# Scalings of k and q on GpSimd from slot 10 on, each as two instructions of 256 columns in place of one of 512

## The chip, the cores and the metric

The kernel runs on one core of a Trainium2 chip. The metric is the device time of one execution in microseconds, as the median of several runs; lower is better. The engines are named as in the profile: PE is TensorE (matmuls), PEld its weight loads, DVE is VectorE, ACT is ScalarE, POOL is GpSimd, SP is the engine whose queue issues nearly all the transfers.

## The reference

The input is q, k and v of shape (4, 8, 768, 64) (batch, heads, sequence, head dimension), and three weight matrices in float32. First a retention layer with a decay per head, then a bilinear feed-forward block:

```python
gamma = 1.0 - 2.0 ** (-5.0 - np.arange(H, dtype=np.float32))
for t in range(S):
    state = gamma * state + outer(k[:, :, t], v[:, :, t])
    y[:, :, t] = scale * (q[:, :, t] @ state)
...
x = y.transpose(0, 2, 1, 3).reshape(3072, 512)
out = ((x @ w_a) * (x @ w_b)) @ w_out      # 512 -> 1536 -> 512
```

## The kernel before, in words

**Tiling.** The 4 x 768 positions are cut into 24 slots of 128 positions. The decay is split into a factor for each position of k and one for each position of q (tables `ktab` and `qtab`, computed once), so that a slot needs: scaled and cast copies of k and q (`kqb`, bf16), a cast of v (`vb`), the transposes of `kqb` (`kqT`), the scores with their mask (`aT`), the running state (`sums`, cast to `gst`), and the output `xt`, which is the input of the feed-forward block. The feed-forward works on blocks J = 0 to 7 of 4, 2, 2, 2, 2, 4, 4 and 4 slots.

**One block.** For each of twelve slices `ft` of 128 hidden columns TensorE computes `a` (line 598) and `g` (line 610), ScalarE casts `a` to `asb` (line 602), and VectorE multiplies `g` by `asb` into `ht` (line 613). Blocks 2 to 7 then compute the output product by a scheme with fewer matmuls (`ffn_fast`, matmuls at line 772), for which four sums and differences of parts of `ht` are formed: `hsum` (line 670), both inputs in SBUF, 128x256 or 128x512 bf16. VectorE does these in blocks 2 to 5 and partly later, GpSimd does most of them in blocks 6 and 7. The results leave PSUM through `snap` (ScalarE, line 784) and `osb` (VectorE, lines 787 and 820). Blocks 6 and 7 use such a scheme for `a` too: it needs combinations of the weights, `ta`, which GpSimd forms after the last slot's casts (line 690) and TensorE reads at line 712, and combinations of `xt`, `xs` (line 681, VectorE).

**Order.** Every engine's instructions are chained in the order in which the program emits them, so each engine works through a fixed list. The recurrence of later slots is put into the blocks by a table of visits, `ahead`: `(casts, t)` emits the casts of slot t, and `(turn, new, old)` the state updates and scores of two new slots (lines 287 and 317) and the outputs of two old ones (lines 359 and 371). For GpSimd only the order of its own list counts, and the waits for data and buffers.

**Casts of one slot** (`casts`, line 246): GpSimd scales k, then q, by `scaled` (the instruction at line 239); SP issues the transpose of both (line 252); after an odd slot SP issues the loads of the next pair of slots, k and q of both and then v of both (lines 96 and 98); last GpSimd casts v (line 204). All loads and transposes stand in SP's one queue, in this order. The raw loads have three buffers of two slots, `kqb` and `vb` six buffers of one slot.

**One scaling** works on 128 partitions x 512 columns, which are 8 heads x 64. The source holds the heads in order (two halves r of four heads hp); the destination interleaves the halves, hp before r, so that the transposes come out as the scores need them. The factor is one number for each partition and head, broadcast over the 64 columns. The first slots, up to 9, are scaled by `casts2` and `casts` in the same way, some of them on VectorE.

Of the kernel before, what the change touches and what calls it, by code (L numbers as in the profile page):

```python
# [12 lines left out]
ALU = mybir.AluOpType  # L13
# [14 lines left out]
def kernel(  # L28
# [46 lines left out]
    def seq(bi):  # L75
        ins = bi.ins
        prev = last.get(ins.engine)
        if prev is not None:
            tc.add_manual_dep(ins, prev.name, nosync, reason="program order")
        last[ins.engine] = ins  # L80
        return bi
# [151 lines left out]
    def scaled(eng, t, i):  # L233
        ktab, qtab = tabs[0] if t < 2 * PAIRS else tabs[1]
        dst, src, tab = kqb[t][:, i], raws["kq"[i], t], (ktab, qtab)[i][:, t % NCH]
        dst = dst.rearrange("p hp r d -> p r hp d")
        src = src.rearrange("p (r hp) d -> p r hp d", r=2)
        tab = tab.rearrange("p (r hp) o -> p r hp o", r=2).to_broadcast([P, 2, HP, D])
        seq(eng.tensor_tensor(dst, src, tab, op=ALU.mult))  # L239

    def new_nat(t):
        kqb[t] = nat.tile([P, 2, HP, 2, D], BF16, tag="kqb", name="kqb")
# [3 lines left out]
    def casts(t, names="kqv"):  # L246
        if "k" in names:
            new_nat(t)
            scaled(nc.gpsimd, t, 0)
            scaled(nc.gpsimd, t, 1)  # L250
            kqT[t] = tra.tile([P, 2, HP, P], BF16, tag="kqT", name="kqT", bufs=6)
            seq(nc.sync.dma_start_transpose(
                out=kqT[t].rearrange("p a b c -> p (a b) c"),
                in_=kqb[t].rearrange("p a hp r d -> p (a hp r d)")))
            if t % 2 and t + 1 < NSLOT:
                for names in ("kq", "v"):
                    load_slot(t + 1, names)
                    load_slot(t + 2, names)
        if "v" in names:
            cast(nc.gpsimd, vb[t], raws["v", t])  # L260
# [169 lines left out]
    def casts2(u, on):  # L430
        if 2 * u not in kqb:
            for t in (2 * u, 2 * u + 1):
                new_nat(t)
        for (i, par), eng in on.items():
            t = 2 * u + par
            if i == V:
                cast(eng, vb[t], raws["v", t])
            else:
                scaled(eng, t, i)
# [631 lines left out]
```

## Time and profile before

| | |
|---|---|
| median of 3 runs | 221.41 us (221.08 to 221.74) |
| profiled execution | 221.99 us, span 220.3 us |
| PE busy | 212.1 us (96%) |
| DVE busy | 147.8 us (67%) |
| POOL busy | 116.2 us (53%), 157 instructions |
| ACT busy | 96.6 us (44%) |
| scalings on POOL, k and q | 21 + 21 of 128x512, 22.7 + 22.5 us, mean 1081 and 1076 ns |
| adds of `hsum` on DVE, largest group | 32 instructions, 14.2 us, mean 450 ns |

Times of rows are microseconds from the start of the span unless marked ns. A timeline row gives the start, the time it took (of a merged row, of all its instructions together), the engine, the line, the operation with output and inputs, and in brackets how long the engine idled before it and what ended that. SPq is SP's issue queue. Matmuls overlap, so a row of several is shorter than the sum of their durations. In a row of groups stand busy time, mean ns of one, and idle time before.

### The profile page before, as it was taken

The numbers are of one execution on the slowest core, as the hardware profiler recorded it, in microseconds if no ns is written. First come the engines' busy times: TensorE is split into PE (matmuls) and PEld (weight loads), VectorE is DVE, ScalarE is ACT, GpSimd is POOL, SyncE is SP. The second block draws the span as 40 slices with busy tenths as digits, with TensorE's granted clock in tenths as the row PEclk, the third lists the DMA queues.
The fourth block names the chain that finished last, engine by engine and source line by source line (L and its number), as shares of the span: only waits on it lengthen the run. The fifth ranks groups of instructions, "written<-read, shape, count | busy, mean of one in ns | idle before, by whom it ended". The sixth has DMA issues, their size and how long they took to land.

```text
span 220.3 us, 7032 instructions
## 1 busy us (share of the span) xinstructions
PE 212.1 (96%) x2875; PEld 156.5 (71%) x2875; DVE 147.8 (67%) x324; ACT 96.6 (44%) x240; POOL 116.2 (53%) x157
## 2 busy tenths in 40 slices
PE   8889999999999999999999999999999999999993
PEld 7568898886456888887878445478666478666682
DVE  2774456657806687698685489897877694777731
ACT  3665334442426436426466343636432643443231
POOL 6457798682734545054352514536959960087500
PEclk9999999999999999999999999999999999999999
DMA  6999999997999997997868899898800002200022
GB/s 172 346 377 382 369 299 390 342 207 167 216 259 246 233 220 141 128 236 203 191 130 201 230 150 257 156 221 120 237 0 4 0 3 98 97 0 1 3 95 95
DMA packets 94832, 39.77 MB, mean 181 GB/s; under 512 B 76112, under 2 KB 91728, under 8 KB 94800
## 3 DMA queue, kind: packets, MB, share of 16 engines
q1 hardware_dynamic: 94656, 39.20, 70.2%
q8 instruction: 22, 0.36, 0.7%
q10 hardware_dynamic: 144, 0.13, 0.2%
q14 instruction: 10, 0.08, 0.1%
HBM read 28.31 MB, written 6.29 MB: 157 GB/s over the span
## 4 chain that ended last, share of the span: by engine, by line
PE 86%; DVE 5%; DMA 3%; issue 2%; POOL 1%; ACT 1%; SPq 0%; DVEq 0%; POOLq 0%; ACTq 0%
PE g L610 27%; PE a L598 22%; PE o L772 18%; PE o L647 7%; PE a L712 5%; DMA kf<-in_k_dram 3%; DVE ht L613 2%; DVE hsum L670 1%; PE st L287 1%; POOL kqb L239 1%; PE y L359 1%; PE y L371 1%; PE at L317 1%; PE tp L450 1%; PE st L491 1%
## 5 line engine op out<-in xcount | busy, mean ns | idle before, releaser
L613 DVE TENSOR_TENSOR ht<-g,asb 128x256 bf16<-128x256 f32 (+1 forms) x98 | 53.7, 548 | 39.1 <-PE g L610 29.3
L610 PE MATMUL g<-xt,wb_bf 128*128 128x256 bf16 (+1 forms) x432 | 77.7, 308 | 0.3 <-ACT asb L602 0.3
L598 PE MATMUL a<-xt,wa_bf 128*128 128x256 bf16 (+1 forms) x368 | 60.8, 296 | 0.1
L602 ACT CAST asb<-a 128x256 bf16<-128x256 f32 (+1 forms) x82 | 36.8, 450 | 51.4 <-PE a L598 50.8
L610 PEld LDWEIGHTS <-wb_bf 128*128 128x128 bf16 x432 | 42.1, 98 | 16.5 <-issue 0.4
L598 PEld LDWEIGHTS <-wa_bf 128*128 128x128 bf16 x368 | 35.4, 98 | 12.1
L239 POOL TENSOR_TENSOR kqb<-kf,ktab 128x512 bf16<-128x512 f32 x21 | 22.7, 1081 | 40.5 <-DMA kf<-in_k_dram 29.8
L239 POOL TENSOR_TENSOR kqb<-qf,qtab 128x512 bf16<-128x512 f32 x21 | 22.5, 1076 | 6.4 <-DMA qf<-in_q_dram 6.4
L204 POOL CAST vb<-vf 128x512 bf16<-128x512 f32 x24 | 14.8, 624 | 17.8 <-DMA vf<-in_v_dram 13.0
L772 PEld LDWEIGHTS <-hsum 128*128 128x128 bf16 x216 | 21.0, 98 | 4.1 <-DVE hsum L670 0.9
L784 ACT COPY snap<-o 128x256 f32<-128x256 f32 x34 | 12.7, 374 | 21.3 <-PE o L772 19.5
L772 PE MATMUL o<-wt_bf,hsum 128*128 128x256 bf16 x162 | 19.8, 272 | 0.9 <-DVE osb L787 0.5
L670 POOL TENSOR_TENSOR hsum<-ht 128x256 bf16<-128x256 bf16 (+1 forms) x15 | 11.0, 733 | 17.9 <-DVE ht L613 17.9
L772 PEld LDWEIGHTS <-ht 128*128 128x128 bf16 x162 | 15.4, 98 | 2.6
L647 PE MATMUL o<-wo_bf,ht 128*128 128x512 bf16 x72 | 16.1, 379 | 0.0
L670 DVE TENSOR_TENSOR hsum<-ht 128x256 bf16<-128x256 bf16 (+1 forms) x32 | 14.2, 450 | 0.3
L301 DVE TENSOR_TENSOR sums<-st,sums 128x256 f32<-128x256 f32 x30 | 12.7, 423 | 1.5
L772 PE MATMUL o<-wo_bf,ht 128*128 128x256 bf16 x108 | 13.3, 273 | 0.0
L202 ACT CAST gst<-sums 128x256 bf16<-128x256 f32 x33 | 12.6, 412 | 0.5 <-DVE sums L299 0.3
L647 PEld LDWEIGHTS <-ht 128*128 128x128 bf16 x72 | 6.9, 98 | 7.9
L323 DVE TENSOR_TENSOR aT<-at,mask 128x512 bf16<-128x512 f32 x18 | 12.1, 680 | 0.0
L787 DVE TENSOR_TENSOR osb<-o,snap 128x256 f32<-128x256 f32 x20 | 8.3, 416 | 4.8 <-PE o L772 3.2
(99 smaller groups left out, 260.4 us busy)
## 6 DMA issues: line engine op xcount, KB each, us to landing
out_dram<-osb SPq DMA_DIRECT2D x11, 512.0 KB, 3.2
kf<-in_k_dram SPq DMA_DIRECT2D x18, 256.0 KB, 3.9
qf<-in_q_dram SPq DMA_DIRECT2D x36, 128.0 KB, 3.8
vf<-in_v_dram SPq DMA_DIRECT2D x18, 256.0 KB, 4.2
wsta<-in_moe_w_a_dram SPq DMA_DIRECT2D x6, 512.0 KB, 7.6
wstb<-in_moe_w_b_dram SPq DMA_DIRECT2D x6, 512.0 KB, 7.8
wsto<-in_moe_w_out_dram SPq DMA_DIRECT2D x6, 512.0 KB, 8.7
kf<-in_k_dram SPq DMA_DIRECT2D x3, 512.0 KB, 6.1
```

Source lines behind the costliest of these rows:

```text
L202: seq(nc.scalar.copy(dst, src))
L204: seq(engine.tensor_copy(dst, src))
L239: seq(eng.tensor_tensor(dst, src, tab, op=ALU.mult))
L301: seq(nc.vector.tensor_tensor(new, u[c][:, s], old, op=ALU.add))
L598: seq(nc.tensor.matmul(a[:, b0 - c0 : b1 - c0], wa_bf[:, kt, fs], xcols(J, kt, b0, b1), start=(kt == 0 and b0 == c0), stop=(kt == KT - 1 a ...
L602: seq(nc.scalar.copy(asb, a))
L610: seq(nc.tensor.matmul(g[:, b0 - c0 : b1 - c0], wb_bf[:, kt, fs], xcols(J, kt, b0, b1), start=(kt == 0 and b0 == c0), stop=(kt == KT - 1 a ...
L613: seq(nc.vector.tensor_tensor(ht[J][:, ft, c0:c1], g, asbs.pop((J, ft, c0)), op=ALU.mult))
L647: seq(nc.tensor.matmul(o, ht[J][:, ft, i * P : (i + 1) * P], wo_bf[:, f, 2 * r : 2 * r + 2, :].rearrange("p a d -> p (a d)"), start=(ft == ...
L670: seq(eng.tensor_tensor(s[which], x(), y(), op=op))
L772: seq(nc.tensor.matmul(R[:, :DH], lhs, (wo_bf, wt_bf)[w][:, f, m, :], start=(first and f == 0), stop=(f == NH - 1), skip_group_check=True))
L784: seq(nc.scalar.copy(snap[:, i], R[:, :DH]))
```

## The change

From slot 10 on each scaling is issued as two instructions, one for each half r of the heads: four heads, 256 columns. The views are the ones that the single instruction used, with the index r taken out. Both functions that emit casts call `scaled`, but `casts2` handles only slots 0 to 5, so the 14 slots 10 to 23, with two scalings each, are affected: 28 instructions become 56. The engine, the order, the number of elements, the transposes and the loads stay as they were.

```diff
         dst = dst.rearrange("p hp r d -> p r hp d")
         src = src.rearrange("p (r hp) d -> p r hp d", r=2)
         tab = tab.rearrange("p (r hp) o -> p r hp o", r=2).to_broadcast([P, 2, HP, D])
-        seq(eng.tensor_tensor(dst, src, tab, op=ALU.mult))
+        if t < 10:
+            seq(eng.tensor_tensor(dst, src, tab, op=ALU.mult))
+        else:
+            for r in range(2):
+                seq(eng.tensor_tensor(dst[:, r], src[:, r], tab[:, r], op=ALU.mult))
```

## The prediction

> **What bounds the kernel now.** I read the page first (busy times, then the chain that ended last), then a table of windows for TensorE's idle time, then the timeline where it idles.
>
> ```profile
> PE 212.1 (96%) x2875; PEld 156.5 (71%) x2875; DVE 147.8 (67%) x324; ACT 96.6 (44%) x240; POOL 116.2 (53%) x157
> ...
> PE g L610 27%; PE a L598 22%; PE o L772 18%; PE o L647 7%; PE a L712 5%; DMA kf<-in_k_dram 3%; DVE ht L613 2%; DVE hsum L670 1%; PE st L287 1%; POOL kqb L239 1%; PE y L359 1%; PE y L371 1%; PE at L317 1%; PE tp L450 1%; PE st L491 1%
> ```
>
> TensorE is the bound, 212.1 of 220.3 us. GpSimd has half its span free, so its own work is not the point. What the change can win is TensorE's idle time where the scalings of slots 10 to 23 run, from about 66 to 153 us. The windows that hold nearly all of it (columns: window, its length, then TensorE, weight loads, DVE, ACT and POOL busy us with counts, clock, DMA share, GB/s):
>
> ```profile
> 93.00:97.00 4.00, 3.69 (x51) 3.09 (x48) 3.58 (x9) 1.68 (x5) 2.09 (x2) 1.00 1.05 235
> 97.00:102.00 5.00, 4.63 (x142) 3.90 (x143) 4.69 (x12) 2.44 (x7) 3.27 (x4) 1.00 0.88 234
> ...
> 109.00:116.00 7.00, 6.73 (x170) 5.54 (x172) 6.27 (x16) 4.07 (x13) 3.68 (x5) 1.00 0.71 147
> ...
> 144.00:150.00 6.00, 5.51 (x156) 4.58 (x155) 5.32 (x13) 1.78 (x6) 2.17 (x2) 1.00 1.05 237
> ```
>
> Idle: 0.31 + 0.37 us around the end of block 3, 0.27 in block 4, 0.49 at the end of block 5; the granted clock is 1.00 throughout, so nothing here is throttling. The timeline of the first place, all engines:
>
> ```profile
> 90.74 0.28 DVE L670 TENSOR_TENSOR hsum<-hsum,ht 128x256 bf16<-128x256 bf16 x1
> ...
> 93.74 1.04 POOL L239 TENSOR_TENSOR kqb<-kf,ktab 128x512 bf16<-128x512 f32 x1 [5.72 <-DMA kf<-in_k_dram]
> 93.84 1.09 DVE L670 TENSOR_TENSOR hsum<-ht 128x256 bf16<-128x256 bf16 x1
> ...
> 94.77 1.06 POOL L239 TENSOR_TENSOR kqb<-qf,qtab 128x512 bf16<-128x512 f32 x1
> ...
> 95.19 0.79 DVE L670 TENSOR_TENSOR hsum<-hsum,ht 128x256 bf16<-128x256 bf16 x1
> ...
> 96.99 0.45 PE L287 MATMUL st<-vb,kqb 64*64 64x64 bf16 x32 [0.31 <-DVE ht L613]
> ...
> 98.76 1.04 POOL L239 TENSOR_TENSOR kqb<-kf,ktab 128x512 bf16<-128x512 f32 x1
> ...
> 99.27 0.68 DVE L670 TENSOR_TENSOR hsum<-ht 128x256 bf16<-128x256 bf16 x1
> ...
> 99.76 1.09 POOL L239 TENSOR_TENSOR kqb<-qf,qtab 128x512 bf16<-128x512 f32 x1
> ...
> 99.98 1.01 DVE L670 TENSOR_TENSOR hsum<-hsum,ht 128x256 bf16<-128x256 bf16 x1
> ...
> 101.06 1.15 PE L772 MATMUL o<-wt_bf,hsum 128*128 128x256 bf16 x8 [0.37 <-DVE hsum L670]
> ```
>
> See how an add of `hsum` that meets nothing takes 0.28 us, and how one that starts inside a scaling ends just after it: 93.84 + 1.09 = 94.93, when the scaling from 93.74 ended at 94.78; 95.98 against 95.83; 99.95 against 99.80; 100.99 against 100.85. The add is held until the GpSimd instruction is over, then needs 0.15 us more. It is let in even though the next scaling stands ready and starts at 94.77. TensorE then waits for the products of these adds (101.06), or for the `ht` behind them in VectorE's order (96.99). The second place:
>
> ```profile
> 145.26 1.04 POOL L239 TENSOR_TENSOR kqb<-kf,ktab 128x512 bf16<-128x512 f32 x1 [4.77 <-PE o L772]
> ...
> 145.30 1.15 DVE L670 TENSOR_TENSOR hsum<-hsum,ht 128x256 bf16<-128x256 bf16 x1
> ...
> 146.76 1.12 POOL L239 TENSOR_TENSOR kqb<-qf,qtab 128x512 bf16<-128x512 f32 x1 [0.45 <-DMA qf<-in_q_dram]
> 146.90 1.33 DVE L670 TENSOR_TENSOR hsum<-ht 128x256 bf16<-128x256 bf16 x2
> ...
> 148.56 0.41 DVE L787 TENSOR_TENSOR osb<-o,snap 128x256 f32<-128x256 f32 x1
> ...
> 149.02 1.47 PE L772 MATMUL o<-wt_bf,hsum 128*128 128x256 bf16 x12 [0.49 <-DVE osb L787]
> ```
>
> Here the held adds push back `osb` at 148.56, which has to free a bank before TensorE goes on at 149.02.
>
> **The change, part by part.** It removes 28 scalings of 512 columns (slots 10 to 23, k and q) and adds 56 of 256. Same bytes, same order, no new wait, no DMA issue moved; the transposes behind them on SP still wait for the last instruction of q.
>
> *Price of one split.* The trace has no scaling of 256 columns. The nearest rows are two-input adds on POOL in both sizes:
>
> ```profile
> 166.84 1.15 POOL L670 TENSOR_TENSOR hsum<-ht 128x512 bf16<-128x512 bf16 x1
> 167.95 1.15 POOL L670 TENSOR_TENSOR hsum<-ht,hsum 128x512 bf16<-128x512 bf16 x1
> ...
> 169.81 0.67 POOL L670 TENSOR_TENSOR hsum<-hsum,ht 128x256 bf16<-128x256 bf16 x1
> 170.44 0.67 POOL L670 TENSOR_TENSOR hsum<-ht 128x256 bf16<-128x256 bf16 x1
> ```
>
> Start to start 1.11 us for 512 columns and 0.63 for 256, so two halves cost 1.26 - 1.11 = 0.15 more; I take 0.14, as the next add follows 0.62 later. Bounds: 0 below (time by columns alone), and 0.19 above, by the rows' own durations (2 x 0.67 - 1.15). A scaling is 1.00 start to start (85.43 to 86.43 below), so a half is about 0.57. In all 28 x 0.14 = 3.9 us more on POOL, which has 104 us free.
>
> [...]
>
> *Where the price lands.* The scalings sit in a loop that paces itself:
>
> ```profile
> 84.86 0.61 POOL L204 CAST vb<-vf 128x512 bf16<-128x512 f32 x1 [2.37 <-DMA vf<-in_v_dram]
> 85.43 1.04 POOL L239 TENSOR_TENSOR kqb<-kf,ktab 128x512 bf16<-128x512 f32 x1
> 86.43 1.04 POOL L239 TENSOR_TENSOR kqb<-qf,qtab 128x512 bf16<-128x512 f32 x1
> ...
> 87.50 1.23 SPq L252 DMA_TRANSPOSE kqT<-kqb  x1
> ...
> 88.78 1.96 SPq L98 DMA_DIRECT2D kf<-in_k_dram  x1
> ```
>
> The cast of the even slot's v waits for its load; the odd slot's k and q follow (85.43, 86.43); when q ends at 87.47, SP issues the transpose (87.50), and then the loads of the next pair (88.78), for which POOL waits (93.74, 5.72 us). The even slot's splits hide in the wait for v, the odd slot's do not: each round is 0.28 us longer. Slots 10/11 to 22/23 make seven rounds, so slot 14's scalings start 2 x 0.28 = 0.56 us later, slot 22's 6 x 0.28 = 1.7, and what follows slot 23 on POOL, the `ta` combinations, 7 x 0.28 = 1.96. Is that covered?
>
> ```profile
> 153.46 0.67 POOL L690 TENSOR_TENSOR ta<-wa_bf 128x256 bf16<-128x256 bf16 x1
> ...
> 156.36 0.84 POOL L690 TENSOR_TENSOR ta<-wa_bf 128x256 bf16<-128x256 bf16 x1
> ...
> 157.83 0.38 PE L712 MATMUL a<-xs,ta 128*128 128x256 bf16 x2
> ...
> 160.86 0.38 PE L712 MATMUL a<-xs,ta 128*128 128x256 bf16 x2
> ```
>
> The first combination is ready at 154.13 and used at 157.83, that of the next block at 157.20 and used at 160.86: slack 3.7 us. A lag of 1.96 plus a TensorE that arrives 0.9 earlier uses 2.9 of it. Cost: nothing, with 0.8 left; without that cover each us of lag is one of TensorE.
>
> *What it gives back.* A held add waits for the rest of a half, not of a whole. All the held adds shown began in the first half of a scaling: after 0.10, 0.42, 0.51 and 0.22 us at the first place, 0.04 and 0.14 at the second. Each would get free 1.00 - 0.57 = 0.43 earlier: 4 x 0.43 = 1.7 us of VectorE at the first place, 2 x 0.43 = 0.86 at the second, more than the 0.68 and 0.49 that TensorE idles. But the lag changes who meets whom. At the first place the scalings move back 0.56 us: the add of 93.84 then runs free, and the later ones meet other halves. I take two thirds of the 0.68 idle: 0.45. At the second place slot 22's scalings move to about 147.0 and 148.5, behind most of the adds: I take all 0.49. Block 4's 0.27 I leave. Bounds: 0 if the meetings only move; at the top all 1.17 plus the matmul tails that the windows count as busy:
>
> ```profile
> L772 PE MATMUL o<-wt_bf,hsum 128*128 128x256 bf16 x162 | 19.8, 272 | 0.9 <-DVE osb L787 0.5
> ```
>
> One matmul lasts 0.27 and twelve take 1.47 (149.02), so they start (1.47 - 0.27) / 11 = 0.11 apart and a stall hides 0.16 of tail; three stalls give 0.5, together 1.7.
>
> **Sum.** -0.45 - 0.49 + 0 = -0.94 us. The profiled execution took 221.99 (span 220.3, 1.7 around it) and would take 221.05. It lies 0.58 above the median of the runs, 221.41, so for the median I say 221.41 - 0.94 = 220.5.
>
> **Rivals.**
>
> *The meetings only move.* Free adds at one place become held ones at another; block 3's stall shrinks by a quarter of what I say and block 4 gets one. For it: the lag of up to 1.96 us shifts every scaling against VectorE's adds. Against it: at the second place it shifts them off the adds. 0.2 us gained: 221.2.
>
> *The add is not let in between the halves.* Then a scaling holds it for 1.13 us in place of 1.00, 0.13 more for each of six held adds, of which about half reach TensorE: 0.4 us, 221.8. Against it: the add of 93.84 ended at 94.93, inside the scaling that followed without a gap.
>
> *Everything comes back*, tails too: 1.7 us, 219.7. For it: VectorE wins 2.6 us at the two places. Against it: not all adds there run free.
>
> *Slower: the loop's lag outgrows the cover of `ta`.* The lag is 14 splits x s, where s is the price of one plus the time that an add let in between takes from POOL. TensorE then waits for the first `ta`, and what it won before is lost in that wait, so the end moves by 14 s - 3.7: nothing is left of the gain from s = 0.26 on, and it is slower by over 0.66 us from s = 0.31. At s = 0.38 (twice the upper bound) the end is 5.3 - 3.7 = 1.6 us later: 223.0. For it: adds at the seams push back the second half. Against it: the scaling of 99.76, at whose start an add got in, took 1.09, only 0.05 over 1.04. [...]
>
> **How the numbers follow.** A measurement of this kernel can tell about 0.3%, 0.66 us, from no change: faster is below 220.75, slower above 222.07. Forecast 0.46; everything comes back 0.11; meetings only move 0.24; not let in 0.07; slower 0.12. So faster 0.57, same 0.31, slower 0.12. The forecast's own range is 219.9 to 220.8. To leave out no more than 2 in 10 the range goes down to 219.5, just past the full gain, and up to 221.9, over the two cases of no change; the slower case stays outside.
>
> **What would show it.** POOL with 56 scalings of 128x256 and a mean near 0.61 us. Held adds of `hsum` at 0.4 to 0.6 us, none near 1.1. The idle of 101.06 and 149.02 gone or halved. Slot 22's k scaling 1 to 2 us later against the span's start, and the first `ta` likewise, while the first L712 on `ta` starts with no wait. I am wrong if adds still end with the second half, if TensorE waits for `ta`, or if VectorE is early at both places and TensorE idles there as before, on something else.

## The result and the profile after

The changed kernel takes 219.65 us (median, 219.44 to 220.27) against 221.28 us (221.08 to 221.74) for the kernel before, measured beside it. The ratio is 0.9941, 95% interval 0.9918 to 0.9963: faster by 0.4 to 0.8%. The profiled execution took 220.27, its span 218.6. The page of the changed kernel (all lines below line 239 have moved down by 4):

```profile
PE 211.2 (97%) x2875; PEld 155.8 (71%) x2875; DVE 147.0 (67%) x324; ACT 96.5 (44%) x240; POOL 120.7 (55%) x185
...
L243 POOL TENSOR_TENSOR kqb<-kf,ktab 128x256 bf16<-128x256 f32 x28 | 17.1, 631 | 33.3 <-DMA kf<-in_k_dram 33.3
```

GpSimd has 28 instructions and 4.5 us of busy time more (120.7 against 116.2), and the whole is shorter all the same. Where the time went is read best from the chain of waits: the times at which it reaches a new block. The kernel before, first matmul of `a` in blocks 3, 4, 5, behind the combinations in block 6, and in block 7 (columns: start, length, what):

```profile
85.92 0.44 PE a L598 x4
...
103.51 0.44 PE a L598 x4
...
121.67 0.86 PE a L598 x4
...
155.82 1.73 PE a L598 x8
...
187.43 1.73 PE a L598 x8
```

The same five places in the changed kernel:

```profile
85.52 0.44 PE a L602 x4
...
102.07 0.44 PE a L602 x4
...
120.00 0.86 PE a L602 x4
...
153.57 1.73 PE a L602 x8
...
185.69 1.73 PE a L602 x8
```

Subtract neighbours: block 3 went from 17.59 to 16.55 (-1.04), block 4 from 18.16 to 17.93 (-0.23), the stretch of block 5 from 34.15 to 33.57 (-0.58), that of block 6 from 31.61 to 32.12 (+0.51). Before block 3 the changed kernel is 0.40 ahead, of which 0.27 is there already at the start of block 2 (69.43 and 69.16), a few us after the first split (slot 10's k, 65.05), so most of it is not the change's. With the last stretch (32.87 and 32.91) these make up the 1.7 us between the spans. Below, the times of blocks in other profiles are read in this way.

The windows of the changed kernel that answer to those shown of before, and one in block 6:

```profile
93.00:97.00 4.00, 4.00 (x136) 3.50 (x136) 3.73 (x10) 1.66 (x5) 2.47 (x4) 1.00 1.03 232
97.00:102.00 5.00, 5.00 (x79) 4.49 (x73) 4.64 (x11) 3.56 (x10) 3.66 (x6) 1.00 1.10 212
109.00:116.00 7.00, 6.74 (x188) 5.50 (x190) 6.21 (x17) 4.27 (x14) 4.01 (x7) 1.00 1.00 140
144.00:150.00 6.00, 6.00 (x164) 5.24 (x162) 4.81 (x15) 2.64 (x8) 2.37 (x4) 1.00 0.87 195
170.00:187.00 17.00, 16.64 (x180) 11.67 (x179) 12.62 (x31) 7.42 (x19) 8.19 (x13) 1.00 0.09 33
```

TensorE's idle time at the end of blocks 3 and 5 is gone, the 0.26 in block 4 is as it was, and block 6 has 0.36 new. The timeline of the changed kernel at the first place:

```profile
93.30 1.23 POOL L243 TENSOR_TENSOR kqb<-kf,ktab 128x256 bf16<-128x256 f32 x2 [5.21 <-DMA kf<-in_k_dram]
93.44 0.63 DVE L674 TENSOR_TENSOR hsum<-ht 128x256 bf16<-128x256 bf16 x1
94.32 0.36 DVE L674 TENSOR_TENSOR hsum<-hsum,ht 128x256 bf16<-128x256 bf16 x1
...
94.51 1.26 POOL L243 TENSOR_TENSOR kqb<-qf,qtab 128x256 bf16<-128x256 f32 x2
...
98.15 1.23 POOL L243 TENSOR_TENSOR kqb<-kf,ktab 128x256 bf16<-128x256 f32 x2
98.37 0.54 DVE L674 TENSOR_TENSOR hsum<-ht 128x256 bf16<-128x256 bf16 x1
...
98.94 0.59 DVE L674 TENSOR_TENSOR hsum<-hsum,ht 128x256 bf16<-128x256 bf16 x1
...
99.29 2.13 PE L776 MATMUL o<-wt_bf,hsum 128*128 128x256 bf16 x18
...
99.34 1.28 POOL L243 TENSOR_TENSOR kqb<-qf,qtab 128x256 bf16<-128x256 f32 x2
```

See the add of 93.44: it ends at 94.07, in the middle of the two halves that run from 93.30 to 94.53. It was let in at the seam. These adds still meet the scalings, but lose about 0.3 us each (0.54 to 0.63 against 0.28 alone) where they lost 0.4 to 0.8, and the matmuls of 99.29 run through: the bracket that stood at 101.06 in the kernel before is gone. What the adds cost GpSimd is small: here a pair of halves that meets adds takes 1.23 to 1.28 us, a pair that meets none 1.18 (70.50, shown further down).

At the second place the adds no longer meet anything: they are over before slot 22's k starts.

```profile
144.67 0.48 DVE L674 TENSOR_TENSOR hsum<-ht,hsum 128x256 bf16<-128x256 bf16 x2
145.08 0.42 DVE L791 TENSOR_TENSOR osb<-o,snap 128x256 f32<-128x256 f32 x1
...
146.36 1.18 POOL L243 TENSOR_TENSOR kqb<-kf,ktab 128x256 bf16<-128x256 f32 x2 [4.62 <-DMA kf<-in_k_dram]
```

Last the combinations, which the prediction had as the price, and the new stall of block 6:

```profile
154.06 0.80 DVE L685 TENSOR_TENSOR xs<-xt 128x512 bf16<-128x512 bf16 x1 [0.78 <-POOL kqb L243]
154.54 0.85 POOL L694 TENSOR_TENSOR ta<-wa_bf 128x256 bf16<-128x256 bf16 x1
...
155.57 0.38 PE L716 MATMUL a<-xs,ta 128*128 128x256 bf16 x2
...
177.04 0.71 POOL L694 TENSOR_TENSOR ta<-wa_bf 128x256 bf16<-128x256 bf16 x1
177.14 1.43 DVE L674 TENSOR_TENSOR hsum<-ht 128x256 bf16<-128x256 bf16 x2
...
180.95 1.47 PE L776 MATMUL o<-wo_bf,ht 128*128 128x256 bf16 x12 [0.36 <-DVE osb L791]
```

The first `ta` is ready at 155.39 and used 0.18 us later: of the 3.7 us of slack nearly nothing is left. In block 6 two adds last 1.43 us, and 0.48 in the kernel before, as they now run against the later combinations of `ta` (the last ends at 178.42, the two adds at 178.57). The loss is the one known from the scalings, with another partner, and TensorE waits 0.36 us for the `osb` behind them.

### The profile page after: what moved, and what is told of

Same layout as the page of the kernel before. It is cut to its first block, busy times and chain, and to the rows that moved or that the text cites. A ratio compares the mean times of both kernels' runs of the same rounds, so it can differ in the third digit from the quotient of the medians.

```text
span 218.6 us, 7060 instructions
## 1 busy us (share of the span) xinstructions
PE 211.2 (97%) x2875; PEld 155.8 (71%) x2875; DVE 147.0 (67%) x324; ACT 96.5 (44%) x240; POOL 120.7 (55%) x185
## 4 chain that ended last, share of the span: by engine, by line
PE 86%; DVE 4%; DMA 3%; ACT 2%; POOL 1%; issue 1%; SPq 0%; DVEq 0%; POOLq 0%
PE g L614 27%; PE a L602 21%; PE o L776 17%; PE o L651 7%; PE a L716 6%; DMA kf<-in_k_dram 3%; DVE ht L617 2%; PE y L363 1%; POOL kqb L240 1%; PE at L321 1%; PE y L375 1%; PE st L291 1%; DVE hsum L674 1%; PE y L533 1%; PE tp L454 1%
## 5 line engine op out<-in xcount | busy, mean ns | idle before, releaser
L614 PE MATMUL g<-xt,wb_bf 128*128 128x256 bf16 (+1 forms) x432 | 77.9, 308 | 0.4 <-ACT asb L606 0.4
L243 POOL TENSOR_TENSOR kqb<-kf,ktab 128x256 bf16<-128x256 f32 x28 | 17.1, 631 | 33.3 <-DMA kf<-in_k_dram 33.3
L243 POOL TENSOR_TENSOR kqb<-qf,qtab 128x256 bf16<-128x256 f32 x28 | 16.9, 622 | 1.2 <-DMA qf<-in_q_dram 1.2
L240 POOL TENSOR_TENSOR kqb<-kf,ktab 128x512 bf16<-128x512 f32 x7 | 8.2, 1179 | 8.8 <-DMA kf<-in_k_dram 4.9
L674 DVE TENSOR_TENSOR hsum<-ht 128x256 bf16<-128x256 bf16 (+1 forms) x32 | 12.6, 397 | 0.3
```

The source lines that it names most:

```text
L243: seq(eng.tensor_tensor(dst[:, r], src[:, r], tab[:, r], op=ALU.mult))
L614: seq(nc.tensor.matmul(g[:, b0 - c0 : b1 - c0], wb_bf[:, kt, fs], xcols(J, kt, b0, b1), start=(kt == 0 and b0 == c0), stop=(kt == KT - 1 a ...
L674: seq(eng.tensor_tensor(s[which], x(), y(), op=op))
```

## The experiments

Two theories stood against each other. **H, the shorter hold:** the adds get free earlier because a GpSimd instruction is shorter. **S, moving in time:** the extra time on GpSimd moves the scalings to places where they meet fewer adds; any delay would do it. The times of each kernel, with the kernel before run beside it on the same chip (220.8 to 221.2 us):

| kernel | us | ratio, 95% interval |
|---|---|---|
| delay, new scratch tile | 230.86 | 1.0458 (1.0412 to 1.0503) |
| delay, tile that is there | 221.03 | 0.9998 (0.9971 to 1.0025) |
| slots 14, 15 alone | 220.34 | 0.9972 (0.9949 to 0.9995) |
| quarters from slot 10 | 225.49 | 1.0189 (1.0146 to 1.0232) |
| GpSimd writes only | 219.47 | 0.9948 (0.9923 to 0.9973) |
| changed kernel, second time | 219.86 | 0.9937 (0.9909 to 0.9966) |
| changed kernel, third time | 219.98 | 0.9964 (0.9934 to 0.9994) |
| later combinations moved | 219.77 | 0.9938 (0.9913 to 0.9963) |
| odd slots alone | 223.36 | one run |
| v later, 512 columns | 224.11 | 1.0137 (1.0100 to 1.0174) |
| v later, 256 columns | 221.30 | 1.0015 (0.9992 to 1.0038) |
| v later, 128 columns | 219.66 | 0.9938 (0.9916 to 0.9960) |

**A delay without a split, first try.** Scalings of 512 columns, each followed by a clear of a small new tile.

```
+    idle_pool = const.tile([P, 64], BF16, name="idle_pool")
 ...
         seq(eng.tensor_tensor(dst, src, tab, op=ALU.mult))
+        if t >= 10:
+            seq(nc.gpsimd.memset(idle_pool, 0.0))
```

> All scalings stay at 512 columns; after each one from slot 10 on GpSimd clears a scratch tile of 64 columns (0.15 us by the 128x64 memset row of the kernel before), so that its loop lags by about the 0.28 us a round that the splits cost, with the instructions still 1.0 us long. Theory H (the halves help because a held add waits for a shorter instruction): block 3's held adds stay near 1 us and its stall stays; only block 5's place can gain, because slot 22 moves behind its adds. 220.8 to 221.5 against 221.28 before. Theory S (the gain comes from moving the scalings in time): the changed kernel's time, 219.4 to 220.2.

230.86 us, far outside both expectations, and late before the first clear runs: slot 10's k starts at 71.92 instead of 66.28. What the transfers moved, in GB/s by 40 slices of the span, in the kernel before:

```profile
GB/s 172 346 377 382 369 299 390 342 207 167 216 259 246 233 220 141 128 236 203 191 130 201 230 150 257 156 221 120 237 0 4 0 3 98 97 0 1 3 95 95
```

And with the new tile:

```profile
GB/s 172 290 330 351 347 277 360 382 196 146 192 257 187 235 259 192 89 212 204 160 188 79 214 205 202 226 134 196 91 207 0 3 3 91 97 0 1 3 80 104
```

The loads of the second to the seventh slice run at 277 to 360 where they ran at 299 to 390. The new tile takes 128 bytes in each partition of the pool that is opened first, so it may move the tiles behind it; their addresses were not read. The run says nothing about H and S, and the next one does without a new tile.

**The same delay in a tile that is there.**

```
         seq(eng.tensor_tensor(dst, src, tab, op=ALU.mult))
+        if t >= 10:
+            seq(nc.gpsimd.memset(zero[:, :64], 0.0))
```

> As the run with cleared scratch, but the 64 cleared columns lie in a tile that exists already and is no longer read, so that no address moves: scalings of 512 columns from slot 10 on, each followed by about 0.11 us of clearing, which writes and reads nothing. Theory H (held adds wait for a shorter instruction): adds of about 1 us remain in block 3, its stall of about 1 us too; at most block 5's 0.5 us is gained: 220.2 to 221.2 with 220.8 before. Theory S (moving the scalings in time is the gain): as the changed kernel, 219.2 to 220.0. If the loop itself suffers from the clearing as in the run before: over 225.

221.03, ratio 0.9998: the delay by itself wins nothing. Its timeline in block 3:

```profile
98.77 1.09 POOL L239 TENSOR_TENSOR kqb<-kf,ktab 128x512 bf16<-128x512 f32 x1
...
98.99 1.01 DVE L672 TENSOR_TENSOR hsum<-hsum,ht 128x256 bf16<-128x256 bf16 x1
...
99.90 1.04 POOL L239 TENSOR_TENSOR kqb<-qf,qtab 128x512 bf16<-128x512 f32 x1
...
100.06 1.80 PE L774 MATMUL o<-wt_bf,hsum 128*128 128x256 bf16 x14 [0.47 <-DVE hsum L672]
```

From k to q it is 1.13 us, so a scaling with its clear is 0.13 longer, close to the price of a split (0.14). The add lasts 1.01 and TensorE waits 0.47 us for it, as it did in the kernel before (0.37). So S falls as the cause of the gain: the changed kernel beside it has 0.9937 (0.9909 to 0.9966), clear of this run's interval (0.9971 to 1.0025). H stands. Where the two meet does matter in single executions: in this profile block 3 takes 17.19 and the stretch of block 5, without a stall, 33.41, but block 4 takes 18.75. The delay need not be what did it, as slot 22's k starts at 145.16, no later than before (145.26).

**The two slots that meet block 3 alone.**

```
-        seq(eng.tensor_tensor(dst, src, tab, op=ALU.mult))
+        if not (t in (14, 15)):
+            seq(eng.tensor_tensor(dst, src, tab, op=ALU.mult))
+        else:   # the two halves
```

> Only the scalings of slots 14 and 15 are split, those that meet block 3's adds. Theory H: the 1.0 us that TensorE gains between blocks 3 and 4 in the changed kernel's profile comes whole, block 5's place stays as before: 220.1 to 220.5. Theory S: nearly no lag has been added by then, so nothing moves: 221.0 to 221.5.

220.34, ratio 0.9972: by the medians about half of the gain with a seventh of the splits, as H expected. Block 3 takes 16.44 us in its profile. What H did not expect is that the stall at the end of block 5 is gone as well, though slot 22 is not split:

```profile
144.88 0.48 DVE L674 TENSOR_TENSOR hsum<-ht,hsum 128x256 bf16<-128x256 bf16 x2
...
145.46 1.04 POOL L240 TENSOR_TENSOR kqb<-kf,ktab 128x512 bf16<-128x512 f32 x1 [4.04 <-DMA kf<-in_k_dram]
```

TensorE comes to block 5 1.47 us earlier than in the kernel before (120.20 against 121.67), mostly by what it won in block 3, and VectorE's adds are over at 145.36, just ahead of slot 22's k. So in block 5 it is enough that the two miss each other; an earlier TensorE does that as well as a later loop.

**Quarters.** Four instructions of 128 columns for each scaling from slot 10.

```
+                for h in range(2):
+                    hs = slice(2 * h, 2 * h + 2)
+                    seq(eng.tensor_tensor(dst[:, r, hs], src[:, r, hs], tab[:, r, hs], op=ALU.mult))
```

> Each scaling from slot 10 on as four instructions of 128 columns. The lag grows by 14 x 0.42 = 5.9 us over the rounds in place of 14 x 0.14 = 1.96, so the first ta is 3.9 us later than with halves, where its first use came 0.2 us after it was ready. Theory H with the cover of ta as the limit: held adds at 0.3 to 0.45 us, TensorE waits some 3.7 us for ta, 222.0 to 223.8. If the lag is taken up elsewhere (GpSimd idles before every k): 219.3 to 220.

225.49, ratio 1.0189: slower than either expectation, in the way of the slower rival, but the first thing that comes late isn't `ta`. Two windows of its profile and the piece of its chain that ends TensorE's wait:

```profile
144.00:150.00 6.00, 2.98 (x133) 2.42 (x131) 4.19 (x11) 0.88 (x3) 2.66 (x7) 0.96 0.63 106
150.00:156.00 6.00, 6.00 (x48) 4.83 (x43) 2.55 (x5) 3.06 (x9) 3.02 (x9) 0.76 1.06 239
```

```profile
146.07 3.10 DMA kqT<-kqb
...
149.22 0.32 PE at L323 x16
```

TensorE idles for 3.02 us at the end of block 5: 0.97 for the cast of a v that stands behind late quarters, and 2.05 for transposes of slots whose quarters were finished too late. Then the granted clock is 0.76 over the next 6 us. That costs about 1.4 more: from the first matmul of `o` behind the wait to block 6 it takes 8.05 us (150.03 to 158.08), and 6.64 in the kernel before (149.02 to 155.66). Later it waits for `ta` too (the chain has it at 159.97, the matmul at 160.82).

**GpSimd writes, but reads nothing.** From slot 10 on the scalings are left out and `kqb` is cleared in their place, 512 columns at a time.

```
-        seq(eng.tensor_tensor(dst, src, tab, op=ALU.mult))
+        if t < 10:
+            seq(eng.tensor_tensor(dst, src, tab, op=ALU.mult))
+        else:
+            seq(eng.memset(kqb[t][:, i].rearrange("p hp r d -> p (hp r d)"), 0.0))
```

> Leaves out the scalings from slot 10 on: GpSimd writes zeros into kqb instead, 512 columns, reading nothing, so the recurrence of those slots is not computed; all else runs. Theory H, with a hold that needs a GpSimd instruction which reads SBUF: no add of blocks 2 to 5 is held by these, the stalls of blocks 3 and 5 vanish, ta is early: 218.8 to 219.6, which is what shorter holds can win at most. If any GpSimd instruction holds the adds: adds of about 0.5 us remain and 219.3 to 220.3. Theory S says nothing here, since these writes stand at other times.

219.47, ratio 0.9948, no different from the changed kernel. The time lies in both of the expected ranges, so the adds must decide. Its timeline in blocks 2 and 3:

```profile
74.92 0.61 POOL L204 CAST vb<-vf 128x512 bf16<-128x512 f32 x1
74.95 0.72 DVE L673 TENSOR_TENSOR hsum<-hsum,ht 128x256 bf16<-128x256 bf16 x1
...
99.48 0.98 POOL L242 MEMSET kqb<- 128x512 bf16 x2
...
99.72 0.29 DVE L673 TENSOR_TENSOR hsum<-hsum,ht 128x256 bf16<-128x256 bf16 x1
```

The add of 99.72 starts inside the clears, which run without a gap, and takes 0.29, as alone. The add of 74.95 starts inside a cast of v, which reads, ends just after it and takes 0.72. So in this profile an add is held beside a GpSimd instruction that reads (0.72), and not beside one that is as busy but only writes (0.29). With no hold by these instructions the kernel is no faster than with halves, so in this order halves have won about all that a shorter hold of the scalings can win.

**The give-back in block 6.** The changed kernel, with the combinations 4 and 5 moved behind block 6's first output pair, so that they don't meet its adds.

```
-            if f == 3:
-                combine_a(4)
-                combine_a(5)
 ...
+    ahead[6, "o", 2] = [(fenced, nc.gpsimd), (combine_a, 4), (combine_a, 5)]
```

> The changed kernel, with the last two groups of ta combinations moved behind the first pair of output tiles of block 6 (GpSimd waits there for the last matmul of the pair by an instruction of its own), where GpSimd would be idle. If the half us that the changed kernel gives back in block 6 comes from its adds being held by these combinations: the stall of 0.36 us before the second pair there is gone, 0.4 to 0.7 us under the changed kernel, 218.8 to 219.4. If it comes from TensorE reaching block 6 early, with VectorE behind for another reason: the same as the changed kernel.

> The changed kernel once more, as the yardstick for the runs beside it on this chip: 0.990 to 0.997 of the time before.

219.77, against 219.86 for the changed kernel run beside it: the expected gain isn't there. In the profile of that second run of the changed kernel the stretch of block 6 takes 31.62, with no stall; in that of the third TensorE idles 0.47 us there again. So the 0.51 is not a fixed part of the change's time; it is there in some executions and not in others. The profile with the moved combinations has no stall in block 6, but lost 1.16 in block 4 (19.09 against 17.93). Whether the move wins anything by itself stays open.

**The odd slots alone.** The even slot's splits should hide in the wait for v; this leaves them out.

```
-        seq(eng.tensor_tensor(dst, src, tab, op=ALU.mult))
+        if not (t >= 10 and t % 2 == 1):
+            seq(eng.tensor_tensor(dst, src, tab, op=ALU.mult))
+        else:   # the two halves
```

> Only the odd slots from 11 on are split. If the loop paces itself as forecast, all of the lag comes from these: from slot 10's k to slot 22's the scalings take as long as in the changed kernel (81.3 us in its profile, 79.0 before). If the lag comes from both or from the loads: between the two.

One run, 223.36. TensorE waits for transposes, as with the quarters, but only 0.42 us, and 1.07 for `ta`; in block 4 it idles 0.72. From slot 10's k to slot 22's k it is 81.3 us, as in the first profile of the changed kernel (65.05 to 146.36). But the same distance is 79.0 in the kernel before, 77.0 in the second profile of the changed kernel, 77.9 with the delay. So for one and the same kernel the loop varies by over 4 us (77.0 and 81.3), more than the 1.7 us that the splits were to add; between these two k, its waits for loads to land come to 43.6 us in the first profile of the changed kernel and 36.7 in the second, its other waits to 1.8 and 4.0. The lag can't be read from single profiles, and this run settles nothing about it, nor why its loop ran so late.

**The loop in another order, with three lengths of the instruction.** The cast of an even slot's v is moved behind the odd slot's k and q, so that the loop waits once less in each round. Then the same order with halves and with quarters.

```
-        if "v" in names:
-            cast(nc.gpsimd, vb[t], raws["v", t])
+        if "v" in names and (t < 10 or t % 2):
+            for s in range(t - (t >= 10), t + 1):
+                cast(nc.gpsimd, vb[s], raws["v", s])
```

> The kernel before, with whole scalings of 512 columns, but from slot 10 on GpSimd casts an even slot's v after the odd slot's k and q, so that the odd slot's transposes and the next loads don't wait for that v: by the rows of before about 2 us less in each round of the loop, until buffers bound it. Theory H: the hold is as long as before, the adds near 1 us remain where they meet, only at other places: 0.994 to 1.003 of before. If the loop's lateness was itself the cost (waits for transposes or ta): below 0.993.

> The same order with halves from slot 10 on. Theory H with lag as the price: the gain of the changed kernel without its lag, 0.988 to 0.994 of before, up to 0.4% under the changed kernel. If the lag cost the changed kernel nothing: the same as it.

> The same order with quarters of 128 columns. If quarters lost time only by the loop's lag (TensorE waiting for transposes and ta), the lag of 5.9 us is now covered by the shorter rounds and the shorter hold shows: 0.986 to 0.993 of before. If the number of GpSimd instructions is itself the cost: still over 1.01.

> The changed kernel as the yardstick once more: 0.990 to 0.997 of the time before.

The rounds do get shorter: slot pairs start at 91.11, 102.96, 114.53 and 126.33 with 512 columns, some 11.7 us apart (before: 93.74, 105.62, 118.72, 132.26, some 12.8). But the kernel is slower, 1.0137, which neither theory expected. Now four scalings come in a row (114.53 to 118.87), and block 4's adds run all along them:

```profile
114.83 1.01 DVE L671 TENSOR_TENSOR hsum<-hsum,ht 128x256 bf16<-128x256 bf16 x1
...
117.86 1.16 DVE L671 TENSOR_TENSOR hsum<-ht 128x256 bf16<-128x256 bf16 x1
...
119.70 0.39 PE L773 MATMUL o<-wt_bf,hsum 128*128 128x256 bf16 x2 [1.46 <-DVE hsum L671]
```

With quarters the same adds of the same order:

```profile
114.52 0.37 DVE L677 TENSOR_TENSOR hsum<-hsum,ht 128x256 bf16<-128x256 bf16 x1
...
115.99 0.48 DVE L677 TENSOR_TENSOR hsum<-ht 128x256 bf16<-128x256 bf16 x1
```

In one order, and with more and more work on GpSimd, the ratio goes 1.0137, 1.0015, 0.9938, and TensorE's idle time in the window from 116 to 122 us of the three profiles goes 1.80, 1.15, 0.01. That is H once more, in steps. It also shows that quarters don't lose by themselves; in the first order they lost by coming late. The forecast for the quarters (0.986 to 0.993) was just missed, that for the halves (0.988 to 0.994) by more: it left out that this order makes more adds meet scalings, and that the `ta` combinations, which now come some 10 us earlier (144.63, 142.69 and 144.80), meet block 5's adds. TensorE idles 1.89, 1.70 and 1.15 us there, from 144 to 156. None of the three is clearly faster than the changed kernel. One thing speaks for the part of S that is left: with 512 columns in this order block 3 takes only 16.45 us, as slot 15's scalings (93.22) happen to be over before its late adds (97.92). How long a hold is and whether it comes at a bad moment both count.

The third run of the changed kernel gave 0.9964. Its profile has what the first just missed: slot 17's halves (114.44 to 116.95) meet block 4's last adds, which last up to 0.70 (18.74 us for the block), and TensorE waits 0.53 us for the combination, as its chain shows:

```profile
155.67 0.82 POOL ta L694
...
156.53 0.39 PE a L716 x2
```

## Why the prediction was right and wrong

- **The hold and the seam: right.** An add inside a scaling ends just after the half, and is let in at the seam. The rival by which it isn't is out (93.44, ending at 94.07).
- **The price of a split: right.** Slot 11's k and q in the changed kernel, with nothing in between:

```profile
70.50 1.18 POOL L243 TENSOR_TENSOR kqb<-kf,ktab 128x256 bf16<-128x256 f32 x2
71.64 1.18 POOL L243 TENSOR_TENSOR kqb<-qf,qtab 128x256 bf16<-128x256 f32 x2
```

  1.14 us start to start against 1.00, so 0.14, as taken. With adds let in it is 0.05 to 0.10 more in block 3 (1.23 to 1.28 against 1.18), so 0.19 to 0.24 in all, not far below the 0.26 from which nothing would be left of the gain; the two longest pairs of this profile, 1.35 at 106.91 and 1.41 at 138.44, took 0.17 and 0.23 more.
- **The term of block 3: too small.** "I take two thirds of the 0.68 idle: 0.45" measured 1.04. Two things were wrong in it. A third was held back for new meetings, since the scalings of slot 14 were to come 0.56 us later. In this profile the meetings are the old ones: slot 14's k starts 7.78 us after block 3's first matmul, 7.82 before. That is luck, as the loop reached slot 10, the first that is split, 1.23 us earlier (65.05 against 66.28). The adds are still held (0.54 to 0.63), but VectorE has so much in hand with the shorter holds that none of it reaches TensorE; and in the third profile, where slot 14's k comes at 8.79, block 3 takes 16.45 all the same. And the tails of matmuls, which the windows count as busy, belong to the loss: the prediction worked them out (0.16 for each stall) and then used them for the bound alone. 0.68 + 2 x 0.16 = 1.00 would have come close to it. The kernel with only these two slots split confirms the place, 16.44 us.
- **The term of block 5: right in size** (0.49 forecast; 0.58 in the whole stretch), and in the first profile for the reason given, that the two no longer meet. For that no split of slot 22 is needed, only a shift of one side. In the second profile they do meet (slot 22's k starts at 144.53, and two pairs of adds last 1.32 and 0.90), and TensorE idles only 0.14: there it is the shorter hold that pays.
- **Block 4: 0.23 gained where nothing was forecast** in the first profile and in the second (17.93 both), but 0.58 and 0.93 lost against the kernel before where the loop falls otherwise (18.74; 19.09 with the later combinations moved): there the rival by which the meetings only move is partly true. The 0.26 of idle time in its window is a wait for ScalarE's `asb` and stayed. Where the 0.23 come from was not looked into.
- **The cover of `ta`: forecast 0.8 left, 0.18 measured**, and none in the third profile. The 3.52 us that went were shared out otherwise than forecast. TensorE reads its first `ta` 2.26 earlier (157.83, 155.57), where 0.9 was forecast; `ta` is ready only 1.26 later (154.13, 155.39), where 1.96 was. Two errors partly cancel, and that the cover just held is in part luck. Against the span's start slot 22's k came 1.10 later (145.26, 146.36) and the first `ta` starts 1.08 later (153.46, 154.54). The lag was worked out against the start (1.96); the distance from slot 10 to the first `ta` grew by 2.31 (87.18 to 89.49), which lies within the loop's own scatter. "Cost: nothing" holds only for some executions: in the third, TensorE waits 0.53 for `ta`. The prediction had no term for how far the loop varies by itself.
- **What is late next: named incompletely.** When the loop falls behind further, transposes come late ahead of `ta` (the quarters, 2.05 of the 3.02 us). Also `xs` waits for slot 23's q (0.78 at 154.06), since it takes over a raw buffer. The prediction looked at `ta` alone.
- **Block 6: not forecast at all.** In block 6 VectorE's adds held TensorE up in the first profile (+0.51; there they met the later combinations) and in the third (0.47 us idle), and not in the second (31.62, no stall).

In sum: 1.63 us by the medians of the first comparison, and by the ratios of the three 1.3, 1.4 and 0.8, against 0.94 forecast. The mechanism and both main places were right. The term of block 3 was mis-sized, and the first median, 219.65, comes out at the rival by which everything comes back (219.7). It is not quite that case: blocks 3 to 5 give back 1.85, a little more than its 1.7, and in some executions part is lost again in block 4, in block 6 or at `ta`. Whether it goes with the landing of the loads that GpSimd waits for was not tried.

## What to carry to other kernels

Where VectorE's operations stand still beside long GpSimd instructions that read, as the adds of `hsum` do here (1.09 us beside a scaling of 1.04, 0.28 alone), a shorter GpSimd instruction can let them in at its end (0.63 beside halves, at 93.44): count the holds on the chain, with the matmul tails that the windows hide (by the prediction's estimate 0.16 us a stall), and set them against the added instructions' time in GpSimd's own loop. That loop pays the other side of the bill: halves stayed mostly within what the loop had to spare, quarters in the same order did not (1.0189), and in an order with more to spare they did (0.9938). Before trusting a cover of a few us, compare several profiles of one kernel: here the loop itself varied by more than the change added (77.0 and 81.3 us from slot 10's k to slot 22's, against 1.7).

## What the hardware showed that was not expected

- **A new tile of 128 bytes in each partition cost 4.6%.** With the same clears in a tile that was there already the kernel took 221.03, with the new tile 230.86, and its loads were slower from the second slice on (277 to 360 GB/s in the second to the seventh, 299 to 390 in the kernel before). At which addresses the tiles began was not measured, and no run shows what made the loads slower.
- **GpSimd loses little at the seam.** In block 3 its pair of halves takes only 0.05 to 0.10 us longer when waiting adds, of 0.28 us each alone, are let in (1.23 to 1.28 against 1.18).
- **Behind a stall of about 3 us the work took longer too.** After the 3.02 us without work in the one profile with quarters the granted clock was 0.76 in the following 6 us, and from the first matmul of `o` to block 6 it took 8.05 us, 1.4 longer than the 6.64 before. No other window shown here is below 0.96. That is one stall in one profile, and whether it brought the lower clock was not tried.
